# Float32 projections for pairs 4 to 7, earlier gates for the channel weights, and their low parts on VectorE

## The chip, the cores and the metric

The kernel runs on one core of a Trainium2 chip. The metric is the device time of one execution in microseconds. The kernel before takes 1167.94 us, the median of three runs (1167.78 to 1168.32).

## What is computed

The inputs are q, k and v of shape [8 batches, 8 heads, 576 positions, 64], a feature matrix `w_phi` [64, 128] and four weights of a token and channel mixer. Cut to what matters:

```python
def phi(x):
    proj = einsum('bhsd,df->bhsf', x, w_phi)
    proj = proj - max(abs(proj), axis=-1, keepdims=True)
    return concatenate([exp(proj), exp(-proj)], axis=-1)
q_p, k_p = phi(q), phi(k)
kv, z = einsum('bhsf,bhsd->bhfd', k_p, v), sum(k_p, axis=2)
x = einsum('bhsf,bhfd->bhsd', q_p, kv) / (einsum('bhsf,bhf->bhs', q_p, z)[..., None] + 1e-06)
x = x.transpose(0, 2, 1, 3).reshape(8, 576, 512)
h = maximum(x.transpose(0, 2, 1) @ w_tok1, 0) @ w_tok2      # 576 -> 256 -> 576
u = x + h.transpose(0, 2, 1)
out = u + maximum(u @ w_ch1, 0) @ w_ch2                     # 512 -> 1536 -> 512
```

The weights arrive as 64-bit floats.

## The kernel before

Heads are worked on in pairs: pair `i` is heads 2j and 2j+1 of batch `i // 4`, so pairs 0 to 3 are batch 0, pairs 4 to 7 batch 1, and there are 32 pairs. Most matrix products are made at float32 precision out of the faster float32r format: each operand is split into a high and a low part (`split`, lines 71 to 77), and three matmuls high by high, high by low and low by high are summed (`mm3`, line 79).

**Projections.** `less_max` (line 217) multiplies blocks of 128 positions by `w_phi`, takes the largest magnitude of each row and subtracts it. There are two ways to do it. For pairs below `PLAIN` = 4 (`base` is `D` for the keys, 0 for the queries) the data is loaded by `load_plain` (line 268) into the tiles `pair`, two heads above one another, and a float32 matmul (line 242) against `wz`, in which the other half is zero, gives the projection in PSUM; VectorE takes the maximum (line 252) and subtracts it (line 254), both straight from PSUM. For later pairs `load` (line 261) brings the data into `raw`, and `stack` (line 205) makes a tile whose upper half is the high part (a cast on VectorE, line 212) and whose lower half the low part (a subtraction on GpSimd, line 213). One float32r matmul of 256 columns (line 238) against `wp2` gives two partial products, ScalarE copies one of them (line 245), VectorE adds the other (line 247) and takes the maximum (line 252), and GpSimd subtracts it (line 254). There are five key groups, one shared tail and four query groups for a pair: nine matmuls for the keys, nine for tail and queries. The PSUM tile that the projection is written to depends on the way: the early pairs use banks that the later stages have not taken yet (`ps_a`, `ps_h`), the later pairs `keys` (one buffer) and `rest` (three).

**Weights.** `convert` (line 127) turns a block of a 64-bit weight into the high and low float32r parts: a DMA (line 138), the magnitude on ScalarE (146), four integer steps on VectorE (147 to 150) in the tile `bits`, the high part on ScalarE (74) and the low part as a subtraction on GpSimd (77). There are 7 such conversions for the token weights and 24, all of 128x512, for the channel weights (`rawc`, `bitsc`, `wc_h`, `wc_l`, `wc`). The channel weights are held back by `GATES`: conversion number `n` starts with a tiny copy on GpSimd (line 145) out of `den` (the tile `dn`, written on VectorE at line 443), of which each of the pairs 0 to 3 makes two, one for `k` = 0 and one for `k` = 1; gate number 4 is that of pair 2, `k` = 0. From the ninth conversion on there is no such copy.

**Order.** Five generators emit the program and a small weaver interleaves them by given costs: `keys`, `queries`, `token_stream`, `load_weights`, `channel_stream` (line 647). On top of it the tile framework schedules the instructions of each engine by its own estimates, so a change anywhere moves instructions on every engine. Each engine runs its own queue in order. Channel mixing (`channel_mix`, line 543) multiplies by the first channel weights into `h`, splits the result into `gh` and `gl`, and multiplies these by the second into `acc`; the last converted block is `wc2_11`, in the fourth of the tiles called `late`.

Of the kernel before, what the change touches and what calls it, by code (L numbers as in the profile page):

```python
# [19 lines left out]
NP = H // 2  # L20
# [2 lines left out]
T = 256  # L23
E = 1536
NC_, NE, NT = C // P, E // P, T // P
PLAIN = 4
ROWS = 8
BURST = 8
GATES = [4, 4, 6, 6, 7, 7, 7, 7]
BORROWED = 18  # L30
STAGES = 4
LAST = 15
# [12 lines left out]
def mixer_kernel(ctx, tc, qk, vm, vt, w_phi, w1, w2, wc1, wc2d, out):  # L45
# [81 lines left out]
    def convert(hi, lo, srcs, name, tag=None, gate=None):  # L127

        w, n = hi.shape
        if tag is None:  # L130
            tag = f"late{nstage[0] % STAGES}"
            nstage[0] += 1
        raw = wk.tile([P, 4, 256], U32, tag=tag, name=f"raw{name}", bufs=3 if tag == "xt1" else 1)
        raw = raw.rearrange("p a b -> p (a b)")[:w, :2 * n]
        at = 0
        for src in srcs:
            m = src.shape[1]
            nc.sync.dma_start(raw[:, 2 * at:2 * (at + m)].bitcast(I64), src)
            at += m
        raw = raw.rearrange("p (n two) -> p n two", two=2)  # L140
        top, low = raw[:, :, 1], raw[:, :, 0]
        m = streamed(wk, [P, 512], U32, tag="g", name=f"bits{name}", bufs=4)[:w, :n]

        if gate is not None:
            nc.gpsimd.tensor_copy(m[:, :1].bitcast(F32), gate)
        nc.scalar.activation(m.bitcast(F32), top.bitcast(F32), AF.Abs)
        nc.vector.tensor_scalar(m.bitcast(F32), m.bitcast(F32), LEAST, MOST, op0=ALU.max, op1=ALU.min)  # L147
        nc.vector.tensor_scalar(m, m, 3, 0x3FFFFFF8, op0=ALU.logical_shift_left, op1=ALU.bitwise_and)
        nc.vector.scalar_tensor_tensor(m, top, 0xC0000000, m, op0=ALU.bitwise_and, op1=ALU.bitwise_or)  # L149
        nc.vector.scalar_tensor_tensor(m, low, 29, m, op0=ALU.logical_shift_right, op1=ALU.bitwise_or)  # L150
        split(hi, lo, m.bitcast(F32), nc.scalar, nc.gpsimd)

    def flat(t):
        return t.rearrange("p a b -> p (a b)")
# [1 line left out]
    def turn_of():  # L156


        n = ngated[0]
        ngated[0] += 1  # L160
        g = GATES[min(n, len(GATES) - 1)]
        yield from until(lambda: len(gates) > g)
        return gates[g] if n < len(GATES) else None

    def pace():
        return 1.0
# [47 lines left out]
            out.append(t)  # L214
        return out

    def less_max(ts, units, name, base=None):

        n, kind = len(units), name[0]
        if base == D:
            ps = ps_a.tile([P, 2, 2, F], F32, tag=f"a{nplain['k'] % 2}", name=f"pp{name}")
            nplain["k"] += 1
        elif base == 0 and (nplain["q"] % 2 == 0 or nplain["q"] >= BORROWED):
            ps = ps_h.tile([P, 2, 2, F], F32, tag="h", name=f"pp{name}")
            nplain["q"] += 1
        elif base == 0:
            ps = ps_w.tile([P, 2, 2, F], F32, tag="keys", name=f"pp{name}", bufs=1)
            nplain["q"] += 1  # L230
        elif kind == "k":
            ps = ps_w.tile([P, 2, 2, F], F32, tag="keys", name=f"pp{name}", bufs=1)
        else:
            ps = ps_w.tile([P, 2, 2, F], F32, name=f"pp{name}", **REST)
# [44 lines left out]
    def keys():  # L279
        groups = [[(0, 0), (0, 1)], [(0, 2), (0, 3)], [(1, 0), (1, 1)], [(1, 2), (1, 3)], [None]]  # L280
        todo = None
        for i in range(B * NP):
            yield from until(lambda: i < 2 or i - 2 in asked)
            if i < PLAIN:
                load_plain(i)
            else:
                load(i)
            v_sb, queue = vtiles[i % 2], nc.sync if i else nc.scalar
            queue.dma_start(v_sb[:, 0:4].rearrange("p u j d -> p (u j) d")[:, :, :D], vm[i])
            for j in range(2):  # L290
                queue.dma_start(v_sb[j * D:(j + 1) * D, 4, j, :D], vt[i, j])
            plain = D if i < PLAIN else None
            ts = pairs[i] if i < PLAIN else stack(raws[i], D, f"k{i}")
            for g, us in enumerate(groups):
                pm = less_max(ts, us, f"k{i}_{g}", plain)
                kp = wk.tile([P, 2, 2, F], F32, tag="kp", name=f"kp{i}_{g}")
                for sg in range(2):
                    nc.scalar.activation(kp[:, :len(us), sg], pm[:, :len(us)], AF.Exp, scale=1.0 - 2.0 * sg)  # L298
                yield 0.22
                if todo:  # L300
                    add_kv(*todo)
                    yield 0.82
                todo = (i, g, us, kp, v_sb)
# [42 lines left out]
    def queries():  # L346
        turned, split_up, row_major = None, None, None
        pieces = [(i, k, j) for i in range(B * NP) for k in range(2) for j in range(2)] + [None] * 3
        for piece in pieces:
# [16 lines left out]
            if piece:  # L366
                i, k, j = piece
                if (k, j) == (0, 0):
# [7 lines left out]
                            load(i + 1)  # L376
                        ts = stack(raws[i + 1], 0, f"q{i}")
                    asked.add(i)
                    tail = less_max(ts, [None], f"t{i}", plain)
                    yield 0.11  # L380
                pm = less_max(ts, [(j, 2 * k), (j, 2 * k + 1)], f"q{i}_{k}{j}", plain)
                turned = (i, k, j, pm, tail)
                yield 0.22

# [231 lines left out]
    def token_stream():  # L616
        for b in range(B):
            for h in range(2):
                yield from until(lambda: b * NP + 2 * h + 1 in attended and (b > 0 or PLAIN - 1 in kvs))
                yield from token_mix(b, h, xts[b])  # L620
            mixed.add(b)

# [68 lines left out]
```

## Time and profile before

| | |
|---|---|
| median of three runs | 1167.94 us |
| the profiled execution | 1168.64 us |
| its span, first to last instruction | 1166.6 us |
| TensorE matmul busy (PE) | 1121.0 us, 96% |
| VectorE busy (DVE) | 824.1 us, 71% |
| ScalarE busy (ACT) | 496.7 us, 43% |
| GpSimd busy (POOL) | 573.7 us, 49% |
| mean granted TensorE clock | 0.985 of full speed |

The profile shows one execution. PEld is TensorE's weight load, which overlaps its matmuls; SP is the engine that issues most DMAs. A float32 matmul shows as two records, a float32r one as one record. The names of tiles stand without their numbers, so `ppk<-wz,pair` is any key projection from a `pair` tile. `idle before` is time in which the engine had nothing to run, and the arrow names what ended it.

### The profile page before, as it was taken

How to read it: one execution, taken by the hardware profiler on the slowest of the kernel's cores; microseconds unless marked ns; L12 is line 12 of the kernel's file. 1: busy time of each engine (PE TensorE's matmuls, PEld its weight loads, DVE VectorE, ACT ScalarE, POOL GpSimd, SP SyncE). 2: the span in 40 equal slices, each digit the busy share in tenths (PEclk: the TensorE clock that was granted, in tenths of full speed). 3: DMA queues.
4: the chain of work that ended last, by engine and by line, in shares of the span. 5: the costliest groups of instructions: out<-in, count | busy, mean ns of one | idle time of the engine just before them, and what ended most of it. 6: DMA issues, size and time to landing. Idle time of an engine off the chain costs nothing.

```text
span 1166.6 us, 24295 instructions
## 1 busy us (share of the span) xinstructions
PE 1121.0 (96%) x9208; PEld 1097.5 (94%) x9208; DVE 824.1 (71%) x1767; ACT 496.7 (43%) x1437; POOL 573.7 (49%) x727
## 2 busy tenths in 40 slices
PE   9997589999999999999999999999999999999998
PEld 8986489998999899999999999999999999999998
DVE  7689996458768777878878576684787878763111
ACT  5565454345444445444545343443443445431110
POOL 2266676257455555556646363563564665430000
PEclk9998599999999999999999999999999999999999
DMA  7433530111111111111111011110111110000000
GB/s 205 117 83 108 156 119 14 37 43 38 31 50 31 28 34 39 32 50 31 32 49 32 20 31 48 32 49 10 41 41 41 36 46 12 19 1 19 19 19 19
DMA packets 65460, 54.39 MB, mean 47 GB/s; under 512 B 44800, under 2 KB 56576, under 8 KB 65344
## 3 DMA queue, kind: packets, MB, share of 16 engines
q1 hardware_dynamic: 63824, 52.41, 15.6%
q8 instruction: 73, 1.20, 0.4%
q10 hardware_dynamic: 1520, 0.43, 0.2%
q14 instruction: 43, 0.35, 0.1%
HBM read 43.38 MB, written 9.44 MB: 45 GB/s over the span
## 4 chain that ended last, share of the span: by engine, by line
PE 81%; DVE 12%; issue 3%; POOL 2%; ACT 2%; DMA 0%; DVEq 0%; ACTq 0%; POOLq 0%
PE h L83 25%; PE acc L83 24%; PE pkv L323 9%; PE pn L83 6%; PE ph L83 3%; PE pa L83 3%; PE pt L392 3%; PE ppk L238 2%; PE ppq L238 2%; PE pr L430 1%; DVE bitsc L149 1%; DVE bitsc L147 1%; DVE qh L76 1%; PE px L504 1%; DVE bitsc L150 1%
## 5 line engine op out<-in xcount | busy, mean ns | idle before, releaser
L83 PE MATMUL acc<-gh,wc 128*128 128x256 f32 x1728 | 345.3, 284 | 2.4 <-ACT gh L570 2.4
L83 PEld LDWEIGHTS acc<-gh,wc 128*128 128x128 f32 x1728 | 275.9, 188 | 3.2 <-ACT gh L570 3.1
L83 PE MATMUL h<-uh,wc_h 128*128 128x256 f32 x864 | 247.0, 286 | 3.0 <-DVE gl L571 2.9
L83 PE MATMUL h<-uh,wc_l 128*128 128x256 f32 x864 | 246.0, 285 | 0.0
L83 PE MATMUL h<-ul,wc_h 128*128 128x256 f32 x864 | 244.2, 283 | 0.3 <-POOL ul L551 0.3
L83 PE MATMUL acc<-gl,wc 128*128 128x256 f32 x864 | 242.2, 282 | 0.0
L298 ACT ACTIVATE kp<-pmk 128x256 f32<-128x256 f32 (+1 forms) x320 | 109.0, 389 | 159.8 <-POOL pmk L254 148.6
L83 PEld LDWEIGHTS h<-uh,wc_h 128*128 128x128 f32 x864 | 163.6, 190 | 4.5 <-DVE gl L571 2.7
L323 PE MATMUL pkv<-v,kp 128*128 128x65 f32 (+2 forms) x1152 | 159.6, 271 | 7.5 <-ACT kv L332 4.8
L83 PEld LDWEIGHTS h<-ul,wc_h 128*128 128x128 f32 x864 | 163.8, 190 | 0.6 <-POOL ul L551 0.5
L83 PEld LDWEIGHTS h<-uh,wc_l 128*128 128x128 f32 x864 | 163.4, 189 | 0.0
L83 PEld LDWEIGHTS acc<-gl,wc 128*128 128x128 f32 x864 | 162.7, 188 | 0.1
L323 PEld LDWEIGHTS pkv<-v,kp 128*128 128x128 f32 x1152 | 148.8, 192 | 9.7 <-ACT kv L332 5.6
L77 POOL TENSOR_TENSOR ql<-qf,qh 128x320 fp32r<-128x320 f32 (+1 forms) x96 | 88.0, 917 | 103.9 <-DVE qh L76 90.0
L571 DVE SCALAR_TENSOR_TENSOR gl<-h,gh 128x512 fp32r<-128x512 f32 x108 | 73.6, 681 | 87.4 <-ACT gh L570 86.7
L399 ACT ACTIVATE qf<-pt 128x320 f32<-128x320 f32 (+1 forms) x256 | 91.9, 412 | 83.8 <-PE pt L392 69.7
L76 DVE CAST qh<-qf 128x320 fp32r<-128x320 f32 (+1 forms) x192 | 90.6, 488 | 36.1 <-ACT qf L399 30.6
L570 ACT ACTIVATE gh<-h 128x512 fp32r<-128x512 f32 x108 | 65.0, 601 | 117.9 <-PE h L83 116.4
L213 POOL TENSOR_TENSOR stq<-raw,stq 64x512 fp32r<-64x512 f32 (+1 forms) x56 | 83.1, 1484 | 54.8 <-DVE stq L212 45.6
L254 POOL TENSOR_TENSOR pmk<-pk,mxk 128x256 f32<-128x256 f32 (+1 forms) x140 | 85.6, 612 | 37.6 <-DVE mxk L252 33.8
L254 POOL TENSOR_TENSOR pmq<-pq,mxq 128x256 f32<-128x256 f32 x112 | 72.0, 643 | 61.0 <-DVE mxq L252 58.0
L213 POOL TENSOR_TENSOR stk<-raw,stk 64x512 fp32r<-64x512 f32 (+1 forms) x56 | 80.7, 1441 | 43.3 <-DVE stk L212 33.8
(122 smaller groups left out, 2366.9 us busy)
## 6 DMA issues: line engine op xcount, KB each, us to landing
raw<-in_qk SPq DMA_DIRECT2D x27, 576.0 KB, 3.7
rawc<-in_wc SPq DMA_DIRECT2D x24, 512.0 KB, 3.7
v<-in_vm SPq DMA_DIRECT2D x31, 256.0 KB, 3.3
out_x<-xt SPq DMA_DIRECT2D x12, 256.0 KB, 2.1
out_x<-xt SPq DMA_DIRECT2D x16, 192.0 KB, 2.0
raw<-in_w SPq DMA_DIRECT2D x8, 256.0 KB, 4.4
out_x<-xt SPq DMA_DIRECT2D x16, 128.0 KB, 1.8
pair<-in_qk SPq DMA_DIRECT2D x8, 160.0 KB, 4.5
```

Of the source, the lines that this page charges most:

```text
L76: eng_hi.tensor_copy(hi, raw)
L77: eng_lo.tensor_tensor(lo, raw, hi.bitcast(F32), op=ALU.subtract)
L83: nc.tensor.matmul(o, a, m, start=first and i == 0, stop=last and i == 2, skip_group_check=group_ok)
L213: nc.gpsimd.tensor_tensor(t[lo:lo + D], src, t[base:base + D].bitcast(F32), op=ALU.subtract)
L238: nc.tensor.matmul(ps[:, i].rearrange("p two f -> p (two f)"), t[:, c:c + P], wp2.rearrange("p two f -> p (two f)"), start=True, stop=True)
L254: eng.tensor_tensor(pm[:, :n], pr, mx[:, :n].unsqueeze(2).to_broadcast([P, n, F]), op=ALU.subtract)
L298: nc.scalar.activation(kp[:, :len(us), sg], pm[:, :len(us)], AF.Exp, scale=1.0 - 2.0 * sg)
L323: nc.tensor.matmul(o, kp[:, n, sg], v, start=g == 0 and n == 0 and sg == 0, stop=u is None, skip_group_check=True)
L392: nc.tensor.transpose(ptr[:, n], r, ident)
L399: nc.scalar.activation(full, src, AF.Exp, scale=1.0 - 2.0 * sg)
L570: nc.scalar.activation(gh, ph, AF.Relu)
L571: nc.vector.scalar_tensor_tensor(gl, ph, 0.0, gh.bitcast(F32), op0=ALU.max, op1=ALU.subtract)
```

## The change

Pairs 4 to 7 take the float32 way (`PLAIN` is 8), but with the PSUM tiles of the later pairs, since `early` is set for the first `NP` = 4 pairs alone. The gates of the first eight channel-weight conversions move from the pairs 2 and 3 to the pairs 1, 2 and 3. The low parts of all 24 channel-weight conversions are made by VectorE; `turn_of` returns 0 where it returned `None`, so that a conversion without a gate takes VectorE too. The 7 token-weight conversions keep GpSimd.

```diff
-PLAIN = 4
+PLAIN = 8
-GATES = [4, 4, 6, 6, 7, 7, 7, 7]
+GATES = [2, 3, 4, 5, 6, 6, 7, 7]
...
-        if gate is not None:
+        if gate:
             nc.gpsimd.tensor_copy(m[:, :1].bitcast(F32), gate)
...
-        split(hi, lo, m.bitcast(F32), nc.scalar, nc.gpsimd)
+        split(hi, lo, m.bitcast(F32), nc.scalar, nc.gpsimd if gate is None else nc.vector)
...
-        return gates[g] if n < len(GATES) else None
+        return gates[g] if n < len(GATES) else 0
...
-    def less_max(ts, units, name, base=None):
+    def less_max(ts, units, name, base=None, early=False):
         n, kind = len(units), name[0]
-        if base == D:
+        if early and base == D:
             ps = ps_a.tile([P, 2, 2, F], F32, tag=f"a{nplain['k'] % 2}", name=f"pp{name}")
             nplain["k"] += 1
-        elif base == 0 and (nplain["q"] % 2 == 0 or nplain["q"] >= BORROWED):
+        elif early and base == 0 and (nplain["q"] % 2 == 0 or nplain["q"] >= BORROWED):
             ps = ps_h.tile([P, 2, 2, F], F32, tag="h", name=f"pp{name}")
             nplain["q"] += 1
-        elif base == 0:
+        elif early and base == 0:
             ps = ps_w.tile([P, 2, 2, F], F32, tag="keys", name=f"pp{name}", bufs=1)
             nplain["q"] += 1
         elif kind == "k":
...
-                pm = less_max(ts, us, f"k{i}_{g}", plain)
+                pm = less_max(ts, us, f"k{i}_{g}", plain, i < NP)
...
-                    tail = less_max(ts, [None], f"t{i}", plain)
+                    tail = less_max(ts, [None], f"t{i}", plain, i < NP)
...
-                pm = less_max(ts, [(j, 2 * k), (j, 2 * k + 1)], f"q{i}_{k}{j}", plain)
+                pm = less_max(ts, [(j, 2 * k), (j, 2 * k + 1)], f"q{i}_{k}{j}", plain, i < NP)
```

The instruction order shows three places. The first is GpSimd's queue in the middle of the conversions, before. `pmk5_1` is the difference of a key group of pair 5, `xl` and `ul` are low parts that token and channel mixing need, `stq50` is a stacked query half of pair 5.

```order
L254 TENSOR_TENSOR pmk5_1_1254<-pk5_1_1250,mxk5_1_1252 128x256
L145 COPY bitsc2_3_1312<-dn3_1_1210 128x1
L77 TENSOR_TENSOR wc2_0_1066<-bitsc2_0_1216,wc2_0_1066 128x512
L254 TENSOR_TENSOR pmq4_01_1280<-pq4_01_1276,mxq4_01_1278 128x256
L254 TENSOR_TENSOR pmk5_2_1340<-pk5_2_1336,mxk5_2_1338 128x256
L77 TENSOR_TENSOR wc2_1_1225<-bitsc2_1_1228,wc2_1_1225 128x512
L77 TENSOR_TENSOR wc2_2_1259<-bitsc2_2_1262,wc2_2_1259 128x512
L213 TENSOR_TENSOR stq50_1596<-raw6_1571,stq50_1596 64x512
L551 TENSOR_TENSOR ul0_2_1688<-xt0_0_397,uh0_2_1687 128x256
```

The same queue now, from the gate of the same conversion to the first stacked tile in it, which is that of pair 8:

```order
L145 COPY bitsc2_3_1187<-dn3_1_1169 128x1
L77 TENSOR_TENSOR xl0_1_3_1344<-rows0_1_756,xh0_1_3_1343 128x256
L77 TENSOR_TENSOR xl0_1_4_1393<-rows0_1_756,xh0_1_4_1392 128x256
L551 TENSOR_TENSOR ul0_2_1600<-xt0_0_397,uh0_2_1599 128x256
L551 TENSOR_TENSOR ul0_3_1604<-xt0_0_397,uh0_3_1603 128x256
L77 TENSOR_TENSOR xl1_0_0_2163<-rows1_0_1369,xh1_0_0_2162 128x256
L77 TENSOR_TENSOR xl1_0_1_2185<-rows1_0_1369,xh1_0_1_2184 128x256
L213 TENSOR_TENSOR stk80_2565<-raw8_2560,stk80_2565 64x512
```

Where GpSimd had low parts, differences and stacks, only the operands of the mixing are left between the last gate and pair 8.

The second place is VectorE's queue at the ninth conversion (`c1_0_512`), before:

```order
L147 TENSOR_SCALAR bitsc1_0_512_1347<-bitsc1_0_512_1347 128x512
L212 CAST stq50_1596<-raw6_1571 64x512
L148 TENSOR_SCALAR bitsc2_3_1312<-bitsc2_3_1312 128x512
L247 TENSOR_TENSOR pq4_10_1379<-ppq4_10_1374,partq4_10_1377 128x256
L148 TENSOR_SCALAR bitsc1_0_512_1347<-bitsc1_0_512_1347 128x512
L539 TENSOR_TENSOR xt0_0_397<-ph0_1_0_0_1478,xt0_0_397 128x320
L247 TENSOR_TENSOR pk5_3_1424<-ppk5_3_1419,partk5_3_1422 128x256
L149 SCALAR_TENSOR_TENSOR bitsc2_3_1312<-rawc2_3_1310,bitsc2_3_1312 128x512
L252 TENSOR_REDUCE mxq4_10_1381<-pq4_10_1379 128x2
```

And now, from the last integer steps of the conversions around it to its low part:

```order
L252 TENSOR_REDUCE mxk5_3_1442<-ppk5_3_1439 128x2
L149 SCALAR_TENSOR_TENSOR bitsc2_3_1187<-rawc2_3_1185,bitsc2_3_1187 128x512
L252 TENSOR_REDUCE mxq4_10_1329<-ppq4_10_1326 128x2
L148 TENSOR_SCALAR bitsc1_1_512_1268<-bitsc1_1_512_1268 128x512
L77 TENSOR_TENSOR wc1_l_105<-bitsc1_0_512_1229,wc1_h_104 128x512
L150 SCALAR_TENSOR_TENSOR bitsc2_2_1175<-rawc2_2_1173,bitsc2_2_1175 128x512
L254 TENSOR_TENSOR pmk5_3_1444<-ppk5_3_1439,mxk5_3_1442 128x256
```

The casts of line 212 and the additions of line 247 are gone, the subtractions of line 254 and the low parts of line 77 have come.

The third place is the start of SP's queue, before:

```order
L273 DMA pair00_116<-in_qk 64x512
L273 DMA pair01_118<-in_qk 64x640
L276 DMA pair00_116<-in_qk 64x512
L276 DMA pair01_118<-in_qk 64x640
L138 DMA raw1_0_141<-in_w1 128x256 x2
```

And now:

```order
L265 DMA raw8_2560<-in_qk 64x1152
L273 DMA pair00_116<-in_qk 64x512
L273 DMA pair01_118<-in_qk 64x640
L276 DMA pair00_116<-in_qk 64x512
L276 DMA pair01_118<-in_qk 64x640
```

The load of pair 8, the first that is stacked now, has been put ahead of the loads of pair 0; its tile is free from the start.

## Rows read from the trace of the kernel before

**Rows 1.** The page's second part: the busy share of VectorE (DVE) and TensorE (PE) in forty equal slices of the span, 29 us each, in tenths (9 is 90% or more).

```profile
PE   9997589999999999999999999999999999999998
...
DVE  7689996458768777878878576684787878763111
```

**Rows 2.** Busy time of each engine in stretches of the span (from:to in us, length, then for PE, PEld, DVE, ACT and POOL the busy us and the instructions; the last three are the granted TensorE clock, the share of the DMA engines, and GB/s).

```profile
0.00:44.00 44.00, 41.24 (x308) 37.72 (x308) 30.56 (x94) 23.62 (x65) 9.25 (x23) 1.00 0.77 197
44.00:60.00 16.00, 16.00 (x141) 15.44 (x140) 10.31 (x32) 8.49 (x26) 5.67 (x7) 1.00 0.19 55
44.00:190.00 146.00, 118.52 (x862) 109.73 (x862) 133.28 (x261) 78.41 (x202) 92.05 (x92) 0.88 0.32 98
60.00:190.00 130.00, 102.52 (x724) 94.29 (x723) 122.97 (x229) 69.92 (x176) 86.37 (x87) 0.87 0.34 103
92.40:99.20 6.80, 6.22 (x29) 5.80 (x29) 6.52 (x12) 4.48 (x12) 4.84 (x7) 0.50 0.20 60
119.70:147.00 27.30, 17.41 (x70) 15.27 (x71) 26.52 (x51) 12.90 (x32) 16.98 (x15) 0.50 0.49 154
190.00:1167.00 977.00, 961.25 (x8042) 950.04 (x8040) 660.21 (x1412) 394.69 (x1172) 472.38 (x613) 1.00 0.11 32
```

**Rows 3.** Waits of TensorE's matmuls from 60 to 190 us: who waited for whom, us in total, times, longest.

```profile
PE ppk L238 <- DVE pk L247: 8.2, 4, 4.8
...
PE pa L83 <- ACT xh L74: 3.5, 1, 3.5
```

**Rows 4.** Groups of VectorE's instructions in the first 200 us, by line: shape, count, busy us, mean ns of one, and the idle time before them.

```profile
L149 DVE SCALAR_TENSOR_TENSOR bitsc<-rawc,bitsc 128x512 uint32<-128x512 uint32 x24 | 24.6, 1030 | 0.1
L150 DVE SCALAR_TENSOR_TENSOR bitsc<-rawc,bitsc 128x512 uint32<-128x512 uint32 x24 | 21.0, 882 | 0.1
L147 DVE TENSOR_SCALAR bitsc<-bitsc 128x512 f32<-128x512 f32 x24 | 18.8, 786 | 2.6 <-ACT bitsc L146 2.6
L148 DVE TENSOR_SCALAR bitsc<-bitsc 128x512 uint32<-128x512 uint32 x24 | 16.9, 708 | 0.2
L247 DVE TENSOR_TENSOR pk<-ppk,partk 128x256 f32<-128x256 f32 (+1 forms) x20 | 7.7, 383 | 2.9 <-ACT partk L245 2.9
...
L212 DVE CAST stk<-raw 64x512 fp32r<-64x512 f32 (+1 forms) x10 | 7.5, 755 | 1.1 <-PE ppk L238 0.9
...
L254 DVE TENSOR_TENSOR pmk<-ppk,mxk 128x256 f32<-128x256 f32 (+1 forms) x20 | 7.3, 383 | 2.1 <-ACT kp L298 2.0
...
L212 DVE CAST stq<-raw 64x512 fp32r<-64x512 f32 (+1 forms) x7 | 6.7, 963 | 3.0 <-PE ppq L238 3.0
...
L571 DVE SCALAR_TENSOR_TENSOR gl<-h,gh 128x512 fp32r<-128x512 f32 x6 | 4.1, 679 | 0.0
```

**Rows 5.** The four integer steps of the 24 conversions one line at a time: durations in ns, shortest/median/longest, and when the first and the last start.

```profile
L147 DVE TENSOR_SCALAR bitsc<-bitsc x24: 395/726/1750, 62.6 to 184.8; 128x512 f32<-128x512 f32 x24
...
L148 DVE TENSOR_SCALAR bitsc<-bitsc x24: 407/502/1483, 63.2 to 185.6; 128x512 uint32<-128x512 uint32 x24
...
L149 DVE SCALAR_TENSOR_TENSOR bitsc<-rawc,bitsc x24: 674/698/1935, 64.5 to 186.3; 128x512 uint32<-128x512 uint32 x24
...
L150 DVE SCALAR_TENSOR_TENSOR bitsc<-rawc,bitsc x24: 671/685/1766, 66.7 to 188.0; 128x512 uint32<-128x512 uint32 x24
```

**Rows 6.** Four instructions in order of time, two of GpSimd and two of VectorE (start us, duration us, engine, line, operation).

```profile
156.79 1.73 POOL L213 TENSOR_TENSOR stk<-raw,stk 64x640 fp32r<-64x640 f32 x1 [0.50 <-DVE stk L212]
...
157.14 1.94 DVE L149 SCALAR_TENSOR_TENSOR bitsc<-rawc,bitsc 128x512 uint32<-128x512 uint32 x1
...
159.55 2.08 POOL L213 TENSOR_TENSOR stq<-raw,stq 64x640 fp32r<-64x640 f32 x1 [1.03 <-DVE dn L443]
...
160.16 1.75 DVE L147 TENSOR_SCALAR bitsc<-bitsc 128x512 f32<-128x512 f32 x1
```

**Rows 7.** GpSimd's low parts of line 77 between 40 and 200 us, columns as in rows 5: the channel weights and the operands of token mixing.

```profile
L77 POOL TENSOR_TENSOR wc_l<-bitsc,wc_h x12: 1266/1382/1945, 69.1 to 171.9; 128x512 fp32r<-128x512 f32 x12
...
L77 POOL TENSOR_TENSOR xl<-rows,xh x11: 726/735/1188, 45.7 to 198.8; 128x256 fp32r<-128x256 f32 x11
```

**Rows 8.** TensorE in order of time: a float32 projection (four records) and a float32r one (two records). The time is from the first start to the last end.

```profile
9.13 0.61 PE L242 MATMUL ppk<-wz,pair 128*128 128x128 f32 x4
...
200.25 0.40 PE L238 MATMUL ppk<-wp,stk 128*128 128x256 f32 x2
```

**Rows 9.** The last conversion in order of time: its last integer step on VectorE, its high part on ScalarE, its low part on GpSimd; then the first matmul that reads `wc2_11`.

```profile
188.01 0.69 DVE L150 SCALAR_TENSOR_TENSOR bitsc<-rawc,bitsc 128x512 uint32<-128x512 uint32 x1
...
188.74 0.62 ACT L74 CAST wc<-bitsc 128x512 fp32r<-128x512 f32 x1 [0.68 <-DVE bitsc L150]
...
189.43 1.30 POOL L77 TENSOR_TENSOR wc<-bitsc,wc 128x512 fp32r<-128x512 f32 x1 [2.00 <-ACT wc L74]
...
199.57 0.36 PE L83 MATMUL acc<-gh,wc 128*128 128x256 f32 x1
```

**Rows 10.** The gates in order of time: `dn` of pair 1 (`k` = 0) on VectorE, the first two gate copies on GpSimd, and `dn` of pair 3 (`k` = 1), the last gate.

```profile
44.04 0.16 DVE L443 TENSOR_SCALAR dn<-pr 128x4 f32<-128x4 f32 x1 [0.71 <-PE pr L430]
...
60.54 0.29 POOL L145 COPY bitsc<-dn 128x1 f32<-128x1 f32 x2
...
88.65 0.16 DVE L443 TENSOR_SCALAR dn<-pr 128x4 f32<-128x4 f32 x1
```

**Rows 11.** Loads of pairs: SP's wait for the buffer of `raw` in the first 100 us (total, times, longest), and the time from issue to landing of the `pair` loads.

```profile
SPq L265 <- POOL stk L213: 17.3, 2, 11.0
...
DMA to landing us min/median/max: 2.7/4.3/5.9
```

More of the change, by code (lines that the diff above doesn't have):

```diff
@@ L618, in token_stream @@
             for h in range(2):
-                yield from until(lambda: b * NP + 2 * h + 1 in attended and (b > 0 or PLAIN - 1 in kvs))
+                yield from until(lambda: b * NP + 2 * h + 1 in attended and (b > 0 or NP - 1 in kvs))
                 yield from token_mix(b, h, xts[b])
```

## The prediction

> **What bounds the kernel now.** I read the busy slices first. TensorE is at 9 nearly everywhere; the hole lies in slices 3 to 7, and there VectorE shows its 8s and 9s [rows 1]. From 190 us to the end TensorE is busy 961.25 us of the 976.6 us that are left, so that part is TensorE's own and only its order and its amount of work count. The stretch from 60 to 190 us is another case: TensorE is busy 102.52 of 130 us, VectorE 122.97. TensorE's clock falls to half twice inside it, for 6.8 and 27.3 us, while 29 and 70 records run [rows 2]; the falls come behind idle stretches, the longest 3.5 and 4.8 us, in which TensorE waited for ScalarE's high part of a token operand and for VectorE's sum of a key projection [rows 3]. So TensorE loses 27.5 us by idling and, at some 118 ns more for each of the 99 slow records, 11.7 us by the clock: 39.2 us. That is all that the change can win.
>
> What fills VectorE there is the 24 conversions: 24.6 + 21.0 + 18.8 + 16.9 = 81.3 us of busy time [rows 4]. Their durations are odd: one instruction of one shape takes 674 ns at its shortest and 1935 at its longest [rows 5]. The timeline shows why. The 1.94 us one starts at 157.14, while GpSimd is in an instruction that ends at 158.52; it ends 0.56 us behind that. The 1.75 us one at 160.16 ends 0.28 us behind GpSimd's end at 161.63 [rows 6]. The VectorE instruction stands until GpSimd's is over and then does its work. At the shortest durations the 96 steps would take 24 x (395 + 407 + 674 + 671) ns = 51.5 us, so 29.8 of the 81.3 us are blocking.
>
> The end follows from two points. The last converted block is ready at 190.73 us and TensorE first reads it at 199.57 [rows 9]; 967.0 us of the span come behind that read.
>
> **VectorE, part by part, up to the last conversion.**
> The low parts are 24 more instructions of 128x512. VectorE does not do this operation at this shape before. The nearest rows are the step of line 149, also two inputs and 512 columns, at 674 ns unblocked, and `gl` at 679; the upper bound is GpSimd's own 1382 ns. I take 0.68: +16.3 us (bounds 16.2 and 33.2).
> The casts of line 212 go. By the order there are 15 of them ahead of the last conversion before and 1 now; the 17 rows in the first 200 us take 7.5 + 6.7 = 14.2 us, 0.84 each: -11.7 us.
> The additions of line 247 go (31 ahead of the last conversion) and the subtractions of line 254 come in from GpSimd (34 more, of which 3 belong to work that has moved ahead). Both cost 383 ns in the mean [rows 4], and three more maxima move ahead too: +2.2 us.
> Blocking: GpSimd is busy 92.05 us from 44 to 190 [rows 2]. It loses the 24 low parts (1.38 us each), the stacks and the differences of four pairs; by the order 12 low parts for token mixing (0.73 us, [rows 7]), a few of channel mixing and the eight gates stay, some 13.7 us. If the blocking falls with GpSimd's time, 29.8 x 13.7 / 92.05 = 4.4 us stay: -25.4 us. The bounds are 0 and -29.8.
> Sum: 16.3 - 11.7 + 2.2 - 25.4 = -18.6 us. VectorE idles 146 - 133.28 = 12.7 us from 44 to 190, which I leave as it is. The last block is ready at 190.73 - 18.6, about 172 us.
>
> On the blocking the Trainium skill has a rule (SBUF — State Buffer, Who interferes with whom): VectorE and GpSimd share one pair of ports as an exclusive lock, the later one stands still until the earlier one is done, and an instruction with two inputs in SBUF takes part, so the new low parts on VectorE fall under it as well and can hold up GpSimd in turn. The trace agrees for the steps that it shows, with 0.56 and 0.28 us of work behind GpSimd's end; no run yet shows it for the low part.
>
> **The gates.** `dn` of pair 1 is written at 44.04 us, the first gate copies ran at 60.54 and the last gate is written at 88.65 [rows 10]. Four conversions can thus be done in part inside the 16 - 10.31 = 5.7 us that VectorE idles between 44 and 60 us [rows 2]. Of the two low parts and eight steps that fit there I count some 2 us as won: ready at 170 us. GpSimd's gates stand ahead of `xl` of the token mixing in its queue, but those need the rows of the same or an earlier pair, and behind the gate waits nothing else.
>
> **ScalarE** loses the copies of line 245 of four pairs, and each projection one hop between engines. ScalarE waits for others there, so I give it nothing beyond the above.
>
> **TensorE.** Four records of a float32 projection take 0.61 us, two float32r ones 0.40 [rows 8]. With 0.28 us for the last one's own length the step is about 112 ns in the first and 118 in the second, so a projection costs 224 instead of 118 ns: 72 x 106 ns = +7.6 us of TensorE's work, and nothing covers it, since the engine is full to the end. By the order 61 of the float32 projections now stand ahead of the first read of the last block in place of 57 float32r ones (13.7 - 6.7 = +6.9 us), and 18 products, of token mixing and of keys by values but for one, have moved ahead of it (+2.8): 900 instructions have become 922, +9.7 us ahead and -2.1 behind.
> From this side the first read cannot come before 199.57 - 39.2 + 9.7 = 170.1 us, all idling and all half clock gone.
>
> **The start.** The 295 KB load of pair 8 now goes out ahead of pair 0's. At the 197 GB/s of the first 44 us [rows 2] that is 1.5 us of transfer; TensorE's opening work covers part of it. Bounds 0 and 1.5, taken at 1.
>
> **The sum.** Both chains come out at 170 us. They feed one another through single buffers, and before the read came 8.8 us behind the block, so I add 5 us, the late start among them: first read at 175 us. Span: 1166.6 - (199.6 - 175) - 2.1 = 1139.9 us. The profiled execution took 2.0 us more than its span (1168.64 against 1166.6) and lies 0.7 us over the median: 1141.2 us. I say 1141.
>
> **Rivals.**
> *Half of the stall stays.* The low parts wait in VectorE's queue for ScalarE's casts, conversions and projections get in one another's way, TensorE still idles and its clock falls again. For it: TensorE's waits end on ScalarE and VectorE alike [rows 3]. Against it: VectorE, 95% busy, loses 18.6 us. With 19.6 of the 39.2 us left the read comes at 199.6 - 19.6 + 9.7 = 189.7 us, and the time is 1166.6 - 9.9 - 2.1 + 1.3 = 1156 us.
> The Trainium skill (TensorE: Matmul & The Clock Gate, Part 1) says that the low clock is the resting state and that activity lifts it; the trace agrees so far as both falls follow idle stretches.
> *The pair tiles turn too slowly.* A pair of tiles serves pairs i and i+2, so the load of pair 6 can go out only behind the query products of pair 4. By the order 68 records, 8 us, lie between the last such read of the first half and the first key product of pair 6, 6.9 us for pair 7, and landing takes 4.3 us, at most 5.9 [rows 11]. It is hidden unless SP stands at another wait; the longest wait for such a buffer was 11.0 us. Then 11.0 + 4.3 - 8 = 7.3 us each for two pairs: 1156 us too.
> *The long durations stay (the slower side).* If the steps are long for another reason than GpSimd, or the low parts take its place, VectorE gains 16.3 - 11.7 + 2.2 = 6.8 us of work in the stretch in which it is the bound. The block is then ready at 197.5 us, the read comes 6.8 us later, and the time is 1166.6 + 6.8 - 2.1 + 1.3 = 1173 us. It decides as soon as less than 6.8 us of blocking goes. Against it: half of the steps of lines 149 and 150 take 698 and 685 ns or less, close to the shortest [rows 5], and the long ones end at a fixed distance behind GpSimd [rows 6].
> *It does nothing*: the gates are not what held the conversions, and what VectorE wins TensorE's 7.6 us eat. That needs a stall that shrinks by just that much; 1167 us.
>
> **How the numbers follow.** The forecast has 0.64, with a range of its own from 1131 (both chains tight, first read at 165 us, the idle time of 44 to 60 us used up) to 1151 (read at 185). The two rivals at 1156 have 0.21 together, 1173 has 0.10, no change 0.05. The range 1131 to 1160 takes in nearly all of the first and most of the second. A measurement of this kernel tells 0.2%, 2.3 us, from no change. Faster 0.85, same 0.05, slower 0.10.
>
> **What would show it.** Right: the integer steps of the conversions near their shortest durations, a low part at about 0.68 us on VectorE, the last one done near 170 us, TensorE's clock at half for less than the 34.1 us of before, busy time of the matmuls up in the slices 3 to 7. Wrong: steps still at 0.8 to 1.0 us in the mean; or short steps and a last block near 170 us, but a first read far behind it; or waits of TensorE in 60 to 190 us that end on a `pair` load. A later part that loses more than 5 us by its new order would make the time wrong with the mechanism right.

## The result and the profile after

The changed kernel takes 1149.7 us in the median of four runs (1149.39 to 1150.11), the kernel before 1167.86 on the same chip (1167.21 to 1168.32): the ratio is 0.9845, with a 95% interval from 0.9828 to 0.9862. The profiled execution took 1149.39 us, 1147.6 of it span. The forecast was 1141 in a range from 1131 to 1160: the direction and the range held, and of the 27 us forecast 18 came. Two executions in the experiments, one of 1810.65 us with the spread gates and one of 1391.59 us in the first row of the table below, ran at a granted clock of 0.56 and 0.74 and are left out of the ratios.

First the busy slices, which answer to [rows 1]: the hole of TensorE (PE) has shrunk to an 8 and a 7 in slices 4 and 5, and VectorE (DVE) still has its 9s there.

```profile
PE   9998799999999999999999999999999999999998
...
DVE  7779973478687797877787685775777879663111
```

Next the busy time by stretches of the changed kernel, columns as in [rows 2].

```profile
44.00:60.00 16.00, 15.27 (x132) 14.57 (x130) 13.71 (x38) 8.98 (x26) 3.05 (x5) 1.00 0.36 106
60.00:190.00 130.00, 118.89 (x961) 112.76 (x960) 104.22 (x257) 69.29 (x170) 21.73 (x31) 0.99 0.33 103
80.00:100.00 20.00, 16.96 (x141) 15.69 (x140) 18.37 (x43) 11.60 (x30) 6.54 (x6) 1.00 0.34 108
100.00:120.00 20.00, 15.90 (x116) 14.22 (x117) 20.00 (x52) 10.95 (x28) 2.23 (x2) 1.00 0.61 189
120.00:140.00 20.00, 16.03 (x117) 14.63 (x116) 19.07 (x47) 11.80 (x27) 1.89 (x2) 0.91 0.54 175
```

From 60 to 190 us TensorE is busy 118.89 us where it was 102.52. It idles 11.1 in place of 27.5 us, and all of that lies between 80 and 140 us: 3.0 + 4.1 + 4.0. The clock is nearly full. GpSimd (POOL) has fallen from 86.37 to 21.73 us. But in those 60 us VectorE is busy 57.44: it is full where TensorE idles.

The groups of VectorE in the first 200 us, as in [rows 4], show the sizes of the terms.

```profile
L150 DVE SCALAR_TENSOR_TENSOR bitsc<-rawc,bitsc 128x512 uint32<-128x512 uint32 x24 | 17.9, 750 | 0.1
L149 DVE SCALAR_TENSOR_TENSOR bitsc<-rawc,bitsc 128x512 uint32<-128x512 uint32 x24 | 16.9, 713 | 0.1
...
L148 DVE TENSOR_SCALAR bitsc<-bitsc 128x512 uint32<-128x512 uint32 x24 | 10.8, 462 | 0.0
L147 DVE TENSOR_SCALAR bitsc<-bitsc 128x512 f32<-128x512 f32 x24 | 10.7, 448 | 3.6 <-ACT bitsc L146 3.4
L77 DVE TENSOR_TENSOR wc<-bitsc,wc 128x512 fp32r<-128x512 f32 x12 | 8.2, 687 | 0.0
L77 DVE TENSOR_TENSOR wc_l<-bitsc,wc_h 128x512 fp32r<-128x512 f32 x12 | 8.2, 687 | 0.2 <-ACT wc_h L74 0.2
```

The four integer steps take 16.9 + 17.9 + 10.8 + 10.7 = 56.3 us, not 81.3, and the low parts 16.4.

The last conversion in order of time, on three engines, and its first reader, as in [rows 9]:

```profile
163.14 0.69 DVE L150 SCALAR_TENSOR_TENSOR bitsc<-rawc,bitsc 128x512 uint32<-128x512 uint32 x1
```

```profile
163.87 0.62 ACT L74 CAST wc<-bitsc 128x512 fp32r<-128x512 f32 x1 [2.56 <-DVE bitsc L150]
```

```profile
164.97 0.68 DVE L77 TENSOR_TENSOR wc<-bitsc,wc 128x512 fp32r<-128x512 f32 x1
```

```profile
182.34 0.39 PE L83 MATMUL acc<-gh,wc 128*128 128x256 f32 x2
```

The last block is ready at 165.65 us, 25.1 us earlier than before. TensorE reads it at 182.5 (the second record of the last row), 17.1 us earlier than before. Ahead of the change the read followed the block by 8.8 us; now 16.8 us lie between them. The block isn't what the read waits for.

The five longest of the nine groups of waits of TensorE from 60 to 190 us, as in [rows 3]:

```profile
PE ppk L242 <- DVE pmk L254: 2.0, 2, 1.2
PE pr L430 <- ACT qf L399: 1.9, 2, 1.2
PE pf L456 <- DVE rows L445: 1.9, 1, 1.9
PE ppk L242 <- issue: 1.4, 1, 1.4
PE pa L83 <- POOL xl L77: 1.1, 1, 1.1
...
```

No wait on a `pair` load or on a conversion is among the nine. They end on small steps of VectorE and ScalarE that belong to the pairs and, for 2.7 us, on operands of token and channel mixing. One of them, the "issue" of 1.4 us, can be followed. VectorE in order of time in the changed kernel:

```profile
114.34 0.42 DVE L252 TENSOR_REDUCE mxk<-ppk 128x2 f32<-128x256 f32 x1
114.67 0.28 DVE L252 TENSOR_REDUCE mxt<-ppt 128x1 f32<-128x128 f32 x1
114.87 0.68 DVE L150 SCALAR_TENSOR_TENSOR bitsc<-rawc,bitsc 128x512 uint32<-128x512 uint32 x1
115.47 0.42 DVE L252 TENSOR_REDUCE mxq<-ppq 128x2 f32<-128x256 f32 x1
115.80 0.68 DVE L149 SCALAR_TENSOR_TENSOR bitsc<-rawc,bitsc 128x512 uint32<-128x512 uint32 x1
116.40 0.16 DVE L443 TENSOR_SCALAR dn<-pr 128x4 f32<-128x4 f32 x1
116.47 0.68 DVE L77 TENSOR_TENSOR wc_l<-bitsc,wc_h 128x512 fp32r<-128x512 f32 x1
117.07 0.42 DVE L254 TENSOR_TENSOR pmk<-ppk,mxk 128x256 f32<-128x256 f32 x1
```

and TensorE:

```profile
115.77 0.39 PE L323 MATMUL pkv<-v,kp 128*128 128x128 f32 x2
117.59 0.57 PE L242 MATMUL ppk<-wz,pair 128*128 128x128 f32 x3 [1.43 <-issue]
```

The maximum `mxk` and the subtraction `pmk` are of one key projection of pair 6. Between them stand three conversion steps, some 1.9 us of the 2.7. The next projection needs the `ppk` tile that `pmk` reads; it starts 0.1 us behind `pmk`'s end at 117.49, and TensorE has idled 1.43 us. The two waits that end on `pmk` look the same: four conversion steps stand between a maximum at 96.51 us and its subtraction at 99.31, three between 129.42 and 131.89. Over all of the 11.1 us in which TensorE idles, VectorE's records show it in conversion steps for 6.4.

### The profile page after: what moved, and what is told of

Same layout as the page of the kernel before. It is cut to its first block, busy times and chain, and to the rows that moved or that the text cites. A ratio compares the mean times of both kernels' runs of the same rounds, so it can differ in the third digit from the quotient of the medians.

```text
span 1147.6 us, 24293 instructions
## 1 busy us (share of the span) xinstructions
PE 1117.2 (97%) x9280; PEld 1096.4 (96%) x9280; DVE 800.0 (70%) x1775; ACT 485.7 (42%) x1397; POOL 491.1 (43%) x647
## 4 chain that ended last, share of the span: by engine, by line
PE 73%; DVE 10%; POOL 3%; ACT 2%; issue 2%; DMA 1%; SPq 0%; DVEq 0%; POOLq 0%; ACTq 0%
PE acc L83 23%; PE h L83 23%; PE pkv L323 7%; PE pn L83 5%; PE pa L83 3%; PE ph L83 3%; PE pt L392 2%; PE ppk L238 2%; DVE qh L76 2%; PE ppq L238 2%; DVE den L479 1%; DVE ql L77 1%; PE px L504 1%; PE pr L430 1%; DMA rawc<-in_wc 1%
## 5 line engine op out<-in xcount | busy, mean ns | idle before, releaser
L551 POOL TENSOR_TENSOR ul<-xt,uh 128x64 fp32r<-128x64 f32 (+3 forms) x120 | 60.7, 530 | 96.3 <-ACT uh L550 95.7
L83 PE MATMUL pn<-qh,kv 128*128 128x320 f32 (+1 forms) x384 | 99.8, 299 | 0.6 <-DVE qh L76 0.5
L213 POOL TENSOR_TENSOR stk<-raw,stk 64x512 fp32r<-64x512 f32 (+1 forms) x48 | 68.6, 1429 | 70.7 <-DVE stk L212 31.2
L479 DVE RECIPROCAL den<-den 128x320 f32<-128x320 f32 (+1 forms) x48 | 93.5, 1949 | 0.9
```

What stands on the lines that cost most here:

```text
L83: nc.tensor.matmul(o, a, m, start=first and i == 0, stop=last and i == 2, skip_group_check=group_ok)
L213: nc.gpsimd.tensor_tensor(t[lo:lo + D], src, t[base:base + D].bitcast(F32), op=ALU.subtract)
L479: nc.vector.reciprocal(den, den)
L551: nc.gpsimd.tensor_tensor(l[:, d:d + n], t[:, c, o:o + n], h[:, d:d + n].bitcast(F32), op=ALU.subtract)
```

## The experiments

**My theory** after the result: the float32 projections of pairs 4 to 7 carry the gain, through what they take off VectorE and GpSimd, and what is left of the stall is VectorE's full queue between 80 and 140 us, where the conversions stand between the steps of the pairs. **Rivals:** the low parts or the gates carry the gain (the first four runs); TensorE's remaining idling is made of hops between engines, whatever VectorE has to do (the next four).

### One part of the change at a time

Undoing the low parts:

```diff
-        split(hi, lo, m.bitcast(F32), nc.scalar, nc.gpsimd if gate is None else nc.vector)
+        split(hi, lo, m.bitcast(F32), nc.scalar, nc.gpsimd)
```

> The changed kernel with the low parts of the channel weights back on GpSimd. Theory (the pairs' stacks and differences on GpSimd were what blocked VectorE, and their going is the gain): VectorE loses 24 x 0.69 = 16.4 us, GpSimd gains 24 x 1.4 = 33.6 us and blocks some 14 us more of VectorE, so the two about cancel; 1146 to 1154 us. Rival (the low parts on VectorE carry the gain): 1160 us or more.

Undoing the projections:

```diff
-PLAIN = 8
+PLAIN = 4
```

> The changed kernel with pairs 4 to 7 stacked again (PLAIN 4), low parts on VectorE and new gates kept. Theory: 16.3 us of low parts come onto VectorE and take only about 11 us of blocking away, so it is not faster than the kernel before: 1166 to 1175 us. Rival (the low parts carry the gain): 1150 to 1158 us, with the 7.6 us of TensorE's work saved as well.

Undoing the gates:

```diff
-GATES = [2, 3, 4, 5, 6, 6, 7, 7]
+GATES = [4, 4, 6, 6, 7, 7, 7, 7]
```

> The changed kernel with the old gates. Theory: the gates fill some 2 to 5 us of VectorE's idle time between 44 and 60 us and are worth that at most: 1149 to 1155 us. Rival (the earlier conversions carry the gain): 1160 us or more.

Undoing both low parts and gates, so that the projections are alone:

> The kernel before with the float32 projections of pairs 4 to 7 alone (old gates, low parts on GpSimd). Theory: nearly the whole gain, 1148 to 1156 us, in spite of 7.6 us more of TensorE's work. Rivals (low parts or gates carry the gain): 1164 to 1176 us, since TensorE's work grows and nothing else falls.

Measured (the kernel before on that chip: 1168.17 us):

| projections float32 | low parts on | gates | us | ratio, 95% interval | steps, us | last block ready | first read |
|---|---|---|---|---|---|---|---|
| pairs 0 to 3 | VectorE | new | 1169.1 | 1.0005 [0.9996, 1.0015] | 68.1 | 183.2 | 200.6 |
| pairs 0 to 7 | GpSimd | old | 1147.9 | 0.9826 [0.9810, 0.9843] | 66.1 | 174.4 | 182.3 |
| pairs 0 to 7 | VectorE | old | 1148.1 | 0.9826 [0.9811, 0.9840] | 55.9 | 177.4 | 183.8 |
| pairs 0 to 7 | GpSimd | new | 1146.9 | 0.9821 [0.9806, 0.9835] | 65.8 | 166.5 | 181.1 |
| the change | VectorE | new | 1149.7 | 0.9845 [0.9828, 0.9862] | 56.3 | 165.7 | 182.5 |

("Steps" is the sum of lines 147 to 150 in the first 200 us. "Ready" and "read" are us from the start of the span.)

The projections alone give the whole gain, and the low parts and gates without them none. With the projections, neither of the other two parts is worth anything that these runs can tell from nothing; the low parts on VectorE stand 2.8 us to the bad with the new gates and level with the old. The two right columns say why: with eight float32 pairs the last block is ready anywhere between 165.7 and 177.4 us, and the first read stays between 181.1 and 183.8. What finishes conversions sooner buys nothing. Two of the four expectations were missed by a little: with the old gates I expected 1149 to 1155 us and got 1148.1, with the projections alone 1148 to 1156 and got 1147.9.

One rival for the gain itself is left untested. A float32 projection also has fewer steps between load and difference (no cast, no low part, no copy, no addition), so each pair passes through fewer engines. No run here takes work off VectorE in the kernel before without shortening this chain too, so what share of the gain is VectorE's load and what share the shorter chain is not shown.

### More work for GpSimd: does it still hold up VectorE, and does that cost time?

Reading:

```diff
+        if gate is not None:
+            nc.gpsimd.tensor_tensor(wp, ident, m[:, :P].bitcast(F32), op=ALU.add)
+            for _ in range(2):
+                nc.gpsimd.tensor_tensor(wp, ident, wp, op=ALU.add)
```

> The changed kernel with three additions of 128x512... of 128x128 float32 more on GpSimd behind each of the 24 channel conversions, on a tile nobody reads: GpSimd reads both operands in SBUF; the outputs stay as they are. Theory (GpSimd's instructions hold VectorE's steps up while they run): about 72 instructions of 0.4 us, some 29 us more of GpSimd; at the 29.8 / 92.05 us of stalling per busy us read before, VectorE's four steps grow by some 9 us, from 56.3 to 65 us, in L149 and L150 as in L147 and L148. If VectorE's full queue between 80 and 140 us is what keeps TensorE idle there, the time goes up by 4 to 9 us, to 1154 to 1159. Rival (the steps' length no longer sets TensorE's idling): the steps grow, and the time stays at 1150 within 1.5 us. Third: the steps don't grow, and the stalling came from something else that left with the change.

Writing:

```diff
+        if gate is not None:
+            nc.gpsimd.tensor_copy(wp[:, :1], m[:, :1].bitcast(F32))
+            for _ in range(6):
+                nc.gpsimd.memset(wp, 0.0)
```

> As the run before, but what GpSimd does more only writes: one copy of one column and six fills of 128x128 behind each of the 24 conversions, on a tile nobody reads. If it is GpSimd's reading that holds up VectorE's steps with two inputs, the sum of L149 and L150 stays at 34.8 us within 2, and the time at 1150 within 1.5 us; steps with one input (L147, L148) may still grow. If any running instruction of GpSimd holds VectorE up, both pairs of lines grow as in the run before, by the busy time added.

(The additions of the first are of 128x128.) The first took 1155.6 us (ratio 0.9894 [0.9879, 0.9908]), 5.9 over the changed kernel; the second 1149.9 (0.9846 [0.9831, 0.9861]), the same as the changed kernel. GpSimd's added groups and VectorE's low parts, with reads:

```profile
L155 POOL TENSOR_TENSOR wp<-ident,wp 128x128 f32<-128x128 f32 x48 | 29.8, 620 | 3.7
L153 POOL TENSOR_TENSOR wp<-ident,bitsc 128x128 f32<-128x128 f32 x24 | 13.9, 580 | 46.6 <-DVE bitsc L150 42.2 <-issue 3.8
...
L77 DVE TENSOR_TENSOR wc<-bitsc,wc 128x512 fp32r<-128x512 f32 x12 | 10.3, 859 | 0.0
L77 DVE TENSOR_TENSOR wc_l<-bitsc,wc_h 128x512 fp32r<-128x512 f32 x12 | 9.5, 796 | 0.8 <-ACT wc_h L74 0.7
```

and with writes:

```profile
L155 POOL MEMSET wp<- 128x128 f32 x144 | 31.0, 215 | 8.2
L153 POOL COPY wp<-bitsc 128x1 f32<-128x1 f32 x24 | 9.4, 391 | 38.9 <-DVE bitsc L150 32.6 <-issue 3.8 <-DVE pmq L258 2.0
...
L77 DVE TENSOR_TENSOR wc_l<-bitsc,wc_h 128x512 fp32r<-128x512 f32 x12 | 8.2, 682 | 0.8 <-ACT wc_h L74 0.7
L77 DVE TENSOR_TENSOR wc<-bitsc,wc 128x512 fp32r<-128x512 f32 x12 | 8.2, 681 | 0.0
```

GpSimd got 43.7 and 40.4 us more, nearly the same. With reads VectorE's low parts grow from 16.4 to 19.8 us and its integer steps from 56.3 to 60.4, 7.5 us together; with writes the low parts stay at 16.4 and the steps come to 57.8. So it is in the main GpSimd's reading that holds VectorE up: 7.5 us beside reads, 1.5 beside writes (the run with writes reads a little too, in its 24 copies of one column). The Trainium skill says just this (SBUF — State Buffer, Who interferes with whom): an instruction of VectorE with two inputs in SBUF contends with one of GpSimd that reads SBUF, not with one that only writes it. Here the trace agrees, for the low part too, which no run had shown: 0.68 us beside writes, 0.80 and 0.86 beside reads. But of the 4.1 us by which the integer steps grew only 1.4 are on lines 149 and 150, which have two inputs; 2.7 are on lines 147 and 148, which have one and which that rule doesn't name. I had put 9 us on the integer steps alone; they grew by 4.1, and the low parts, which the expectation had left out, by 3.4. And the 7.5 us cost 5.9 us of time, so VectorE's time in the stretch was still what counted. The first read went to 186.9 us.

### Less work for VectorE

```diff
-        nc.vector.tensor_scalar(m, m, 3, 0x3FFFFFF8, op0=ALU.logical_shift_left, op1=ALU.bitwise_and)
+        if gate is None:
+            nc.vector.tensor_scalar(m, m, 3, 0x3FFFFFF8, op0=ALU.logical_shift_left, op1=ALU.bitwise_and)
...
-        nc.vector.scalar_tensor_tensor(m, low, 29, m, op0=ALU.logical_shift_right, op1=ALU.bitwise_or)
+        if gate is None:
+            nc.vector.scalar_tensor_tensor(m, low, 29, m, op0=ALU.logical_shift_right, op1=ALU.bitwise_or)
```

> The changed kernel without the steps of lines 148 and 150 in the 24 channel conversions: the channel weights are then not the reference's. VectorE loses 10.8 + 17.9 = 28.7 us of its work ahead of the last conversion, nothing else changes. Theory (VectorE, 18.4 to 20.0 us busy of each 20 us between 80 and 140, is what still keeps TensorE idle for some 11 us there): most of the idling and of the half clock goes, TensorE first reads wc2_11 at 171 to 175 us in place of 182.5, and the time is 1138 to 1143. Rival (TensorE idles on hops between the engines, from each projection to the softmax and back, whatever VectorE's load): the conversions end 10 us or more earlier, the read stays at 180 or later, and the time is 1147 to 1151.

It took 1141.3 us (ratio 0.9773 [0.9758, 0.9787]), and TensorE first read `wc2_11` at 171.0 us. From 60 to 190 us of this run:

```profile
60.00:190.00 130.00, 125.64 (x1033) 121.10 (x1033) 87.63 (x223) 70.02 (x174) 21.62 (x33) 0.99 0.34 106
```

TensorE idles 4.4 us. Of the 11.1 us 6.7 went with VectorE's load, so hops between the engines aren't the cause of most of it. The granted clock of the stretch is 0.99 in both kernels, so the half clock that the expectation also counted on had no part in it. The theory stands, at both ends: 7.5 us more of VectorE cost 5.9, and 28.7 us less gave 8.4.

### Letting the conversions go later

```diff
-GATES = [2, 3, 4, 5, 6, 6, 7, 7]
+GATES = [2, 3, 4, 5, 6, 6, 7, 7, 7, 7, 7, 7, 8, 8, 8, 8, 9, 9, 9, 9, 9, 9, 9, 9]
...
-        if i < NP:
+        if i < 2 * NP:
             gates.append(den[:, :1])
```

> The changed kernel with the conversions let go later: 24 gates in place of 8, and the gates go on through the pairs of the second half (four conversions behind each of the steps 7 to 9), so that the later conversions don't stand ahead of the second half's softmax in VectorE's queue. Theory (conversions that run early crowd the projections out and so keep TensorE idle between 80 and 140): TensorE idles less, and the time is 1140 to 1146. Rival (the work of VectorE only moves, and the last blocks come later): 1149 to 1156.

It took 1144.1 us (ratio 0.979 [0.977, 0.9809]): faster than the changed kernel, with intervals that don't touch, and the fastest here of those that leave no step out. The last block is ready at 165.2 us, no later than in the changed kernel. By stretches:

```profile
60.00:190.00 130.00, 122.42 (x987) 117.48 (x986) 105.19 (x259) 68.16 (x170) 29.11 (x47) 0.96 0.34 104
...
100.00:120.00 20.00, 15.67 (x100) 14.20 (x100) 20.00 (x51) 10.67 (x26) 5.30 (x8) 0.83 0.63 205
120.00:140.00 20.00, 18.56 (x144) 17.64 (x143) 18.82 (x48) 10.70 (x27) 3.18 (x5) 0.92 0.58 177
```

TensorE's idling falls from 11.1 to 7.6 us, though the clock is lower (0.96), and 987 records fit the stretch in place of 961: 26 more, which at 112 to 118 ns [rows 8] are the 3.0 us by which the first read comes earlier, at 179.5. The rest of the 5 us of span lies behind it (963.1 us for 965.1), which I didn't follow further. VectorE is as full as before between 100 and 120 us: it has the same work, in another order. But the conversions hardly went later. By the records of line 147 the first steps of the 24 conversions start 0.5 us later in the mean than in the changed kernel, 23 of them within 3.1 us of it and one 7.4 us later. So the run shows that another order of the same work is worth 3.0 us up to the first read; it doesn't show that a later start is what pays. The old gates, which let the first steps start 9.5 us later in the mean, gave 1148.1 us for 1149.7, with intervals that overlap.

Two more steps on this version: low parts on GpSimd, and later gates still.

> The spread gates of the run before (24 entries, through the second half's pairs), and the low parts of the channel weights on GpSimd again. VectorE gives up 24 x 0.69 = 16.4 us, GpSimd takes 24 x 1.3 us and may hold VectorE up by up to 9.5 us, as it did with the first eight gates (65.8 us of integer steps in place of 56.3). Theory (VectorE is what TensorE waits for between 80 and 140 us, and 16.4 us less beat 9.5 us of stalling): 1141 to 1143, below 1144.1. Rival (the two come out even now that VectorE is relieved): 1144 within 1 us.

> As the run before, with the later conversions let go later still (two behind each of gates 7 and 8 in place of four, the last four behind gate 10). If what holds TensorE is the crowd of conversions between 100 and 140 us, this thins it further: 1138 to 1141. Rival: the last blocks, done some 20 us ahead of their read so far, become late, and the time is 1144 or more.

The second one's gates:

```diff
+GATES = [2, 3, 4, 5, 6, 6, 7, 7, 7, 7, 8, 8, 8, 8, 9, 9, 9, 9, 9, 9, 10, 10, 10, 10]
```

They took 1145.8 us (0.9813 [0.98, 0.9827]) and 1145.9 us (0.9812 [0.9799, 0.9826]). Neither theory's gain came: where the low parts are made makes no difference that these runs can tell, once more. The last step put the first read at 177.7 us, 6.5 us behind the last block and 1.8 us earlier than the spread gates did; behind the read 966.0 us passed where 963.1 had, so what was won ahead of it was lost again.

### Six float32 pairs

```diff
-PLAIN = 8
+PLAIN = 6
```

> The spread gates with low parts on GpSimd, and only pairs 4 and 5 get float32 projections beside the first four (six in all). TensorE has 36 x 106 ns = 3.8 us less to do; VectorE gets the casts of two pairs back (some 7 us) and GpSimd the stacks of two. Theory (VectorE and its stalling by GpSimd still bind): 3 us or more slower than with eight pairs. Rival (with the conversions spread, VectorE has room): 3 to 4 us faster than with eight.

By an oversight the kernel that ran kept the low parts on VectorE, so it stands beside the 1144.1 us of the spread gates, with only the number of pairs changed; the expectation's text is wrong in that point, its sizes are not. It took 1159.2 us (ratio 0.9929 [0.9915, 0.9942]), 15 us slower for 3.8 us less of TensorE's work. From 60 to 190 us:

```profile
60.00:190.00 130.00, 118.43 (x908) 111.54 (x907) 112.63 (x255) 68.39 (x172) 44.95 (x65) 0.93 0.32 101
```

VectorE has 112.63 for 105.19 us, GpSimd 44.95 for 29.11, and TensorE idles 11.6 for 7.6 us and runs slower (0.93). The first read comes at 185.6 us; 6.1 us are lost ahead of it and 8.1 behind. The sign is that of the theory; what the 8.1 us behind the read are made of stays open.

### The hoisted load

```diff
+        if i == PLAIN:
+            nc.gpsimd.tensor_copy(raw[:, :1], gates[5])
```

> The changed kernel with one edit: the load of pair 8, which had moved ahead of pair 0's, waits for the step of pair 2, so that pair 0's loads are first in the queue as before the change. The prediction charged 1 us for the hoisted load (bounds 0 and 1.5). If it costs that: 1148.2 to 1149.2 and a first projection earlier than 6.4 us. If the load is covered: 1149.7 within 1 us, first projection at 6.4 us.

It took 1151.5 us (0.9859 [0.9845, 0.9872]; 1149.7 to 1152.4), outside both expectations. The first projection began at 7.26 us, at 6.39 in the changed kernel, and at 7.7 us in the run with six pairs, where a load (that of pair 6) was hoisted too. Over the traces with a hoisted load this first start lies between 6.23 and 7.83 us, and in the kernel before, which has none, at 7.72. So the order of the loads doesn't set it by more than it differs from trace to trace, and no gain of putting pair 0 first can be seen. The 1.8 us to the bad, with intervals that overlap, are no price for anything.

## Why the prediction was right, and where it lost 8.7 us

The first read came at 182.5 us where 175 was forecast, which is 7.5 of the 8.7 us; the rest is the distance from the profiled span to the median, 2.1 us where 1.3 was put.

**VectorE's sum.** The low parts were set at +16.3 us and measured 16.4; the blocking at -25.4 and measured -25.0; the casts went, one being left ahead of the last conversion. The gates won more than 2 us: VectorE is busy 13.71 us between 44 and 60 us where it was 10.31, and the table shows the last block 8 and 12 us earlier with the new gates than with the old. The last block was set at 170 us and came at 165.65. The terms for the blocking and the low parts were right; that the sum came so near is luck in part, since with the old gates and the rest of the change the block was ready at 177.4 us, where the sum without the gates gave 172, and the gates then won some six times what was put on them. One reading was too strong: a step doesn't stand until GpSimd's instruction is over and then do all its work, since the 0.56 and 0.28 us behind GpSimd's end are less than the shortest such steps take, 0.674 and 0.395 [rows 5, 6].

**Which edit did it.** My sum had the blocking fall with GpSimd's time, and charged it to the change as a whole. The runs share it out: the float32 projections alone take the steps from 81.3 to 66.1 us, and the casts with them; the move of the low parts takes the steps down to 56.3, but puts 16.4 us on the same engine, and is worth nothing. The proportion itself doesn't carry over: before, 29.8 us were lost to 92.05 of GpSimd, 0.32 for one; with the added reads it was 7.5 for 43.7, 0.17.

**TensorE's floor.** 170.1 us was worked out for the read with no idling and full clock. 11.1 us of idling stay. The clock stands at 0.91 over the 20 us from 120 to 140, so 18% of them, 3.6 us, are at half; at the 11.7 us that 34.1 cost before, that is 1.2. 170.1 + 11.1 + 1.2 = 182.4 us, against 182.5 measured. The 0.7 us that TensorE idles between 44 and 60 us, where before it idled none [rows 2], are not in this sum. So the +7.6 us for float32 and their split hold within about 1 us, and behind the read 965.1 us passed where 964.9 were forecast.

**The step that failed** is "They feed one another through single buffers ... so I add 5 us". It should have been 12.4. I took VectorE's idle time "as it is" and looked at its sum only up to the last block, as if the block's date were the link between the two engines. The link is VectorE's queue: VectorE is busy 57.4 of 60 us between 80 and 140, and in the waits that were followed the softmax step that TensorE waits for stands behind conversion steps that nobody waits for yet. The new gates, which let conversions begin earlier, changed nothing in this. That VectorE's load in this stretch sets TensorE's idling is shown by the run with two steps left out and the one with GpSimd's reads; that the order of the same work counts too, by the spread gates. What the 4.4 us that stay with two steps left out are made of is open.

**The start.** 1 us was charged for the hoisted load; no cost of it can be seen: the first projection started at 6.39 us, before the change at 7.72.

**The rivals.** *Half of the stall stays* lay closest to what happened, and for one of the reasons given there (conversions and projections in one another's way; the clock hardly fell), but 12.4 us and not 19.6 of the 39.2 stayed. *Pair tiles* doesn't appear among the waits. *The long durations stay* is refuted by the groups. Of what was to show the steps right or wrong, the case "short steps and a last block near 170 us, but a first read far behind it" is the one that came.

## What to carry to other kernels

When two engines share a stretch, the date at which one finishes its batch says little; ask what stands in its queue ahead of each small step that the other waits for, and read that from the full slices and not from the sum. A gate that starts background work earlier brings its end forward, but buys no time when that end is not what is waited for: here 8 and 12 us of date were worth nothing. What did pay was less work on the full engine, and another order of the same work, whose rule these runs don't show. Where GpSimd reads SBUF beside a vector engine that is full, count its stalls as vector time, and measure their share anew after each change.

## What was not expected of the hardware

GpSimd seems to be held up in turn: its additions of 128x128 took 450 ns at their shortest and 620 in the mean of the 48, and one copy of a single column 2031 ns where the median was 184. That copy ran beside an unbroken row of VectorE's instructions, the two-input steps among them at their usual 0.66 and 0.69 us. Fills of 128x128, at 215 ns in the mean, ran beside VectorE's two-input steps at almost no cost to them; lines 147 and 148, with one input, grew by 1.2 us together.
